# First token tile turned by TensorE instead of by the DMA: the first 15 microseconds of a matmul-bound kernel

## Chip, cores, metric

One core of one Trainium2 chip. The metric is the device time of one execution in microseconds (us), median over several runs; the kernel before takes 486.51 us (486.48 to 487.02 in its first three runs).

## The reference, cut to what matters

```
x: [2048, 1024] bf16;  two blocks A and B, each with wqkv [1024, 3072] and wo [1024, 1024]
g = sigmoid((x * gate_w).sum(-1))
a = linear attention of x with A's weights;   b = dilated window attention of x with B's weights
out = g * a + (1 - g) * b
```

Everything starts from `x @ wqkv`. The matmuls of this kernel contract over partitions, so they need x transposed: 128 of the 1024 features in the partitions, tokens along the free axis. The input holds x by tokens.

## The kernel before

The program is a list of operations with costs and dependencies; a list scheduler places them and so fixes, before the run, the order of the instructions on every engine. At run time each engine works through its fixed order and waits for semaphores. What matters here is the opening: value projection of block B, token tile by token tile (tile t is 128 tokens), four tiles at a time: first with the left half (512 columns) of the value weights, then with the right half. Eight matmuls of 128x512 make one tile and half.

```python
    WARM = 11
...
        def load_x(t, prio):          # DMA transpose of one token tile, 256 KB, on the sync queue
            return P.op("sp", lambda e: e.dma_start_transpose(xT[:, :, t * 128:(t + 1) * 128], x2[e_, r * 128:(r + 1) * 128, :]),
                        1.5, writes=[...], prio=prio, chan="x%d" % t, lat=1.3)
        def load_w(slot, half, src, c0, prio, d0=0, d1=8, eng="sp", after=()):   # d0..d1: blocks of 128 rows, 128 KB each
            return P.op(eng, lambda e: e.dma_start(ws[slot][:, d0:d1, half * 512:half * 512 + 512], src[:, d0:d1, c0:c0 + 512]), ...)

        load_x(0, 0)
        load_w(0, 0, Bw, 2048, 0.1, 0, 2, "act")
        load_w(0, 0, Bw, 2048, 0.2, 2, 4, "act")
        load_w(0, 0, Bw, 2048, 0.3, 4, 6)
        load_w(0, 0, Bw, 2048, 0.4, 6, 8)
        for t in range(1, NT):
            load_x(t, 3 + t)
        for d in range(0, 8, 2):
            load_w(0, 1, Bw, 2560, 6.1 + 0.1 * d, d, d + 2)
...
        for i in range(WARM):         # matmuls on zeros, to get the TensorE clock released before data arrives
            P.op("pe", lambda e: e.matmul(banks[7].ap(), warm[:, 0:128], warm[:, :], start=True, stop=True), 0.43, ...)
...
            step = 2 if t == 0 else 8  # tile 0 starts on each weight pair as it lands
```

A "weight pair" below is one load of two 128-row blocks, 256 KB. There are four for the left half (two on ScalarE's DMA queue, two on the sync queue) and four for the right half (the "second half's pairs").

## Time and profile before

| | before |
|---|---|
| time, median | 486.51 us |
| span of the profiled run | 485.2 us |
| PE (TensorE) busy | 98% |
| first real matmul | 5.54 us |
| clock of PE released | 4.3 us |
| last pair of the second half landed | 15.02 us |

The first part of the page of before gives busy time, share of the span and number of instructions of each engine; its fourth part, the chain that ended last by engine:

```profile
PE 474.2 (98%) x4339; PEld 222.8 (46%) x4403; DVE 285.2 (59%) x547; ACT 140.2 (29%) x227; POOL 5.9 (1%) x36
...
PE 95%; SPq 2%; issue 1%; DMA 1%; ACT 0%; DVE 0%
```

The list of waits of PE in before, from 15.4 us to the end (what it waited for: us in total, times, longest):

```profile
PE ps_all L1334 <- issue: 3.5, 22, 0.2
PE ps_all L1334 <- DMA w<-in_B_wqkv_dram: 0.3, 1, 0.3
PE ps_all L1334 <- ACT e L1341: 0.2, 1, 0.2
```

Together they say that after the opening PE waits for nearly nothing: what is gained or lost at the start is gained or lost in the whole. The timeline of PE in before, first 20 us (start, duration, instruction, times, and the idle time before it with what ended it; line 1373 is the warm-up, 1334 the projections):

```profile
1.25 4.01 PE L1373 MATMUL ps_all<-warm 128*128 128x512 bf16 x11 [1.25 <-DVE warm L1283]
5.54 1.47 PE L1334 MATMUL ps_all<-w,xT 128*128 128x512 bf16 x6 [0.28 <-DMA xT<-in_A_x_dram]
7.25 0.60 PE L1334 MATMUL ps_all<-w,xT 128*128 128x512 bf16 x2 [0.24 <-DMA w<-in_B_wqkv_dram]
8.17 6.82 PE L1334 MATMUL ps_all<-w,xT 128*128 128x512 bf16 x30 [0.32 <-DMA xT<-in_A_x_dram]
15.30 4.91 PE L1334 MATMUL ps_all<-w,xT 128*128 128x512 bf16 x22 [0.30 <-DMA w<-in_B_wqkv_dram]
```

The clock is best seen in the weight loads of PE (one ahead of each matmul). While the clock is held at half rate they are listed one by one, 0.43 us apart; once it is released they run 0.216 us apart and are merged into one line. In before that happens at 4.2 to 4.4 us, still within the warm-up. The granted-clock column of the page (PEclk) reads 1.00 all the while and does not show it: the trace's own clock records begin only at the first release (4.24 us in before), and what lies ahead of the first record counts as 1.00.

```profile
3.36 0.15 PEld L1373 LDWEIGHTS ps_all<-warm 128*128 128x128 bf16 x1 [0.28 <-issue]
3.79 0.15 PEld L1373 LDWEIGHTS ps_all<-warm 128*128 128x128 bf16 x1 [0.28 <-issue]
4.22 0.55 PEld L1373 LDWEIGHTS ps_all<-warm 128*128 128x128 bf16 x3 [0.28 <-issue]
```

The timeline of the sync queue in before (times in which the queue was busy issuing):

```profile
0.80 1.38 SPq L1308 DMA_TRANSPOSE xT<-in_A_x_dram  x1
2.24 1.06 SPq L1313 DMA_DIRECT2D w<-in_B_wqkv_dram  x2
3.35 4.92 SPq L1308 DMA_TRANSPOSE xT<-in_A_x_dram  x3
8.31 2.12 SPq L1313 DMA_DIRECT2D w<-in_B_wqkv_dram  x4
```

Two more readings of before. First, one window from 3.0 to 5.5 us (busy time of PE, PEld, DVE, ACT, POOL with the number of instructions, then granted clock, DMA share, GB/s): the DMA moves 296 GB/s. Second, the first matmul behind the opening: the key and query projections (`ps_all<-xT,w`), which come after all 16 x 16 = 256 matmuls of the opening, start at 62.1 us.

```profile
3.00:5.50 2.50, 2.26 (x8) 0.70 (x6) 1.03 (x5) 0.06 (x1) 2.08 (x11) 1.00 1.10 296
...
L1334 PE MATMUL ps_all<-xT,w x745: 379/379/390, 62.1 to 389.4; 128*128 128x512 bf16 x187
```

That mark is the ruler of this study. To three digits it is 62.132 us in before. 256 matmuls at 0.2158 us (216 ns start to start, 10.74 us for 49 with the last one's tail) take 55.25 us, so PE stands at the mark as if it had started cleanly, at full rate and without a wait, at 62.13 - 55.25 = 6.89 us. This "clean start" takes in every wait and every slow matmul of the opening. From the mark to the end of the program all profiles of this study take 422.9 to 423.4 us.

### The profile page before, as it was taken

The page shows a single profiled execution, that of the slowest core. Times are in us where ns is not written, and L with a number is a line of the kernel's source. Part 1 is how long each engine was busy: PE and PEld are TensorE (multiplying, and loading weights), DVE is VectorE, ACT ScalarE, POOL GpSimd, SP SyncE. Part 2 cuts the span into 40 slices and gives each one's busy share as a digit, 9 for nine tenths or more (in the row PEclk, how much of TensorE's full clock was granted, in tenths as well). Part 3 has the DMA queues.
Part 4 walks back from the last instruction along what each step waited for, and adds up shares of the span by engine and source line. Part 5 has one row for each costly group of instructions (what it writes and reads, how often), then busy time and mean ns, then how long its engine had stood idle before and what let it go on. Part 6 is the DMA issues. An engine that isn't in the chain of part 4 may idle for free.

```text
span 485.2 us, 10105 instructions
## 1 busy us (share of the span) xinstructions
PE 474.2 (98%) x4339; PEld 222.8 (46%) x4403; DVE 285.2 (59%) x547; ACT 140.2 (29%) x227; POOL 5.9 (1%) x36
## 2 busy tenths in 40 slices
PE   8999999999999999999999999999999999999997
PEld 3444444444444444454544554444444444444443
DVE  2121435888688888665666556496579236653434
ACT  2111121235322234334443333455532230111000
POOL 4000000000000000000000000000000000000000
PEclk9999999999999999999999999999999999999999
DMA  8999993132014459433222322820086018830212
GB/s 224 222 194 299 309 355 122 65 110 86 1 44 135 107 138 245 100 76 86 55 75 67 85 66 66 204 54 2 10 217 163 1 15 242 221 24 2 88 68 89
DMA packets 72951, 57.39 MB, mean 118 GB/s; under 512 B 37953, under 2 KB 60865, under 8 KB 72898
## 3 DMA queue, kind: packets, MB, share of 16 engines
q1 hardware_dynamic: 72210, 56.07, 44.3%
q8 instruction: 36, 0.59, 0.5%
q10 hardware_dynamic: 688, 0.59, 0.4%
q14 instruction: 17, 0.14, 0.1%
HBM read 34.49 MB, written 13.76 MB: 99 GB/s over the span
## 4 chain that ended last, share of the span: by engine, by line
PE 95%; SPq 2%; issue 1%; DMA 1%; ACT 0%; DVE 0%
PE ps_all L1334 78%; PE ps_all L1693 11%; PE ps_all L1463 2%; PE ps_all L1440 2%; SPq L1308 1%; DMA w<-in_B_wqkv_dram 1%; PE ps_all L1556 1%; SPq L1313 1%; PE ps_all L1638 0%; PE ps_all L1610 0%; ACT e L1341 0%; DVE o L1697 0%
## 5 line engine op out<-in xcount | busy, mean ns | idle before, releaser
L1334 PE MATMUL ps_all<-w,xT 128*128 128x512 bf16 x924 | 208.6, 379 | 4.5 <-issue 2.1
L1334 PE MATMUL ps_all<-xT,w 128*128 128x512 bf16 x745 | 166.3, 379 | 2.2 <-issue 1.4
L1334 PEld LDWEIGHTS ps_all<-w,xT 128*128 128x128 bf16 x960 | 91.2, 98 | 111.1 <-DMA w<-in_B_wqkv_dram 2.1
L1334 PEld LDWEIGHTS ps_all<-xT,w 128*128 128x128 bf16 x768 | 73.9, 98 | 88.7 <-issue 1.3
L1693 PE MATMUL ps_all<-w,qT 128*128 128x512 bf16 (+1 forms) x260 | 55.4, 372 | 0.2
L1693 PEld LDWEIGHTS ps_all<-w,qT 128*128 128x128 bf16 x264 | 25.9, 98 | 29.6
L1365 DVE CAST vst<-ps_all 128x512 bf16<-128x512 f32 x15 | 10.4, 694 | 43.5 <-PE ps_all L1334 43.5
L1448 ACT ACTIVATE E<-ps_all 128x1824 bf16<-128x1824 f32 (+1 forms) x18 | 30.4, 1689 | 13.4 <-PE ps_all L1440 13.4
L1345 DVE TENSOR_SCALAR e<-e 128x512 bf16<-128x512 bf16 x64 | 18.4, 290 | 26.9 <-ACT e L1343 14.0
L1697 DVE SCALAR_TENSOR_TENSOR o<-ps_all,gm,xT 128x512 bf16<-128x512 f32 (+1 forms) x25 | 18.0, 728 | 21.1 <-PE ps_all L1693 20.8
L1341 ACT ACTIVATE e<-ps_all 128x512 bf16<-128x512 f32 x32 | 19.1, 598 | 39.0 <-PE ps_all L1334 38.1
L1343 ACT ACTIVATE e<-ps_all 128x512 bf16<-128x512 f32 x32 | 19.1, 598 | 32.3 <-PE ps_all L1334 32.3
L1295 DVE TENSOR_TENSOR mx<-mx,kT 128x1024 bf16<-128x1024 bf16 x32 | 20.9, 688 | 10.9 <-ACT kT L1366 10.8
L1295 DVE TENSOR_TENSOR mx<-mx,qT 128x1024 bf16<-128x1024 bf16 x32 | 20.8, 687 | 7.9 <-ACT qT L1369 7.9
L1451 DVE TENSOR_TENSOR E<-E,msk 128x1824 bf16<-128x1824 bf16 (+1 forms) x18 | 19.9, 1104 | 7.8 <-ACT E L1448 7.4
L1366 ACT ACTIVATE vst<-ps_all 128x512 bf16<-128x512 f32 x17 | 10.2, 601 | 48.5 <-PE ps_all L1334 45.1
L1480 DVE TENSOR_TENSOR ot<-ps_all,rs 128x512 bf16<-128x512 f32 x36 | 23.3, 686 | 0.0
L1366 ACT ACTIVATE az<-ps_all 128x512 bf16<-128x512 f32 x22 | 13.2, 601 | 34.5 <-PE ps_all L1334 34.5
L1366 ACT ACTIVATE kT<-ps_all 128x512 bf16<-128x512 f32 x20 | 11.9, 597 | 37.6 <-PE ps_all L1334 37.6
L1347 DVE SCALAR_TENSOR_TENSOR pk<-ps_all,e 128x512 bf16<-128x512 f32 x32 | 22.0, 689 | 0.7
L1369 ACT ACTIVATE qT<-ps_all 128x512 bf16<-128x512 f32 x19 | 11.4, 598 | 37.4 <-PE ps_all L1334 37.3
L1369 ACT ACTIVATE xT<-ps_all,g 128x512 bf16<-128x512 f32 x10 | 6.9, 689 | 45.1 <-PE ps_all L1334 45.1
(72 smaller groups left out, 260.2 us busy)
## 6 DMA issues: line engine op xcount, KB each, us to landing
rb<-rc_hbm SPq DMA_DIRECT2D x32, 256.0 KB, 5.2
w<-in_A_wqkv_dram SPq DMA_DIRECT2D x6, 1024.0 KB, 9.0
v<-vB_hbm SPq DMA_DIRECT2D x36, 132.0 KB, 2.7
vB_hbm<-vst SPq DMA_DIRECT2D x32, 132.0 KB, 6.2
w<-in_B_wqkv_dram SPq DMA_DIRECT2D x4, 1024.0 KB, 9.5
xn<-in_A_x_dram SPq DMA_DIRECT2D x16, 256.0 KB, 2.7
out_dram<-o SPq DMA_DIRECT2D x15, 256.0 KB, 2.1
oB_hbm<-ot SPq DMA_DIRECT2D x36, 96.0 KB, 2.2
```

Of the source, the lines that this page charges most:

```text
L1295: P.op("dve", lambda e, m=m, op=op: e.tensor_tensor(m[:, 0:n], m[:, 0:n], src, op), 0.08 + n / 1920.0, reads=[m.all(), reg], writes=[m.all()],
L1334: last = e.matmul(bank.ap(), lhs(dc), rhs(dc), start=(dc == 0), stop=(dc == 7))
L1341: P.op("act", lambda e: e.activation(e_[:, :], bank.ap(), ACT.Exp), act(512), reads=[bank.iv], writes=[e_.all()])
L1343: P.op("act", lambda e: e.activation(e_[:, :], bank.ap(), ACT.Exp, accum_out=qe[:, col:col + 1]), act(512) + 0.1, reads=[bank.iv], writes= ...
L1345: P.op("dve", lambda e: e.tensor_scalar(e_[:, :], e_[:, :], 1.0, 1e-6, op0=ALU.min, op1=ALU.add), 0.25, reads=[e_.all()], writes=[e_.all()])
L1347: P.op("dve", lambda e: e.scalar_tensor_tensor(out=dst, in0=bank.ap(), scalar=0.0, in1=e_[:, :], op0=ALU.max, op1=ALU.add), dps(512), read ...
L1366: fa = lambda e: e.activation(dst, src(), ACT.Copy)
L1369: fa = lambda e: e.activation(dst, src(), ACT.Copy, scale=scale)
L1448: P.op("act", lambda e: e.activation(E[:, 0:32 * nq].rearrange("p (j q) -> p j q", j=4), ps[:, 4:8, 0:8 * nq], ACT.Exp), act(32 * nq), rea ...
L1451: P.op("dve", lambda e: e.tensor_tensor(ev(), ev(), m[:, :, :].rearrange("p r q -> p (r q)")[:, None, :].to_broadcast([128, 16, 2 * nq]), ...
L1480: P.op("dve", lambda e, r=r, bv=bv, h=h: e.tensor_tensor(o[:, 512 * h:512 * h + 512].rearrange("p (k i c) -> p k i c", k=2, c=32), bv()[:, ...
L1693: last = e.matmul(bank.ap(0, f1 - f0), qT[:, dc, t * 128:(t + 1) * 128], ws[3][:, dc, f0:f1], start=(dc == 0), stop=(dc == 7))
```

## The change

Intent: do not wait for the slow DMA transpose of tile 0 (5.5 us). Load it by rows in two halves, plain loads at the front of ScalarE's queue, and turn it on TensorE with an identity (8 matmuls of 128 columns into PSUM, four copies by VectorE and ScalarE into `xT`). Tile 1's DMA transpose takes the freed place at the front of the sync queue. Warm-up shrinks from 11 matmuls to 4 and 2 more that fit in where the schedule has room. The rest is for the scheduler: it is told when loads land (`due`), from which it derives the fixed orders.

```diff
-    WARM = 11
+    WARM = 4
+    WARM2 = 2
...
+        def load_x0(lo, hi, prio, pad):
+            P.op("act", lambda e: e.dma_start(x0[:, lo:hi], x2[0, 0:128, lo:hi]), 0.45, ..., lat=None, pad=pad)
+        def due(o, cost, pad):
+            o.cost, o.lat, o.pad = cost, None, pad
-        load_x(0, 0)
-        load_w(0, 0, Bw, 2048, 0.1, 0, 2, "act")
-        load_w(0, 0, Bw, 2048, 0.2, 2, 4, "act")
-        load_w(0, 0, Bw, 2048, 0.3, 4, 6)
-        load_w(0, 0, Bw, 2048, 0.4, 6, 8)
-        for t in range(1, NT):
-            load_x(t, 3 + t)
+        load_x0(0, 512, 0, 1.75)
+        due(load_w(0, 0, Bw, 2048, 0.1, 0, 2, "act"), 0.45, 2.2)
+        load_x0(512, 1024, 0.2, 1.6)
+        due(load_w(0, 0, Bw, 2048, 0.3, 2, 4, "act"), 0.45, 2.1)
+        due(load_x(1, 0), 1.4, 3.9)
+        due(load_w(0, 0, Bw, 2048, 0.3, 4, 6), 0.5, 3.0)
+        due(load_w(0, 0, Bw, 2048, 0.4, 6, 8), 0.5, 3.7)
+        for t in range(2, NT):
+            o = load_x(t, 3 + t)
+            if t < 4:
+                due(o, 1.3, 3.5)
...
+        for p in range(4):            # turn two blocks at a time, copy them into xT
+            def turn(e, b=b, p=p):
+                for k in range(2):
+                    d = 2 * p + k
+                    last = e.matmul(b.ap(128 * k, 128 * k + 128), x0[:, d * 128:(d + 1) * 128], ident[:, :], ...)
+            P.op("pe", turn, 0.22, ...)
+            P.op("act" if p % 2 else "dve", fn, ...)
+        for i in range(WARM2):
+            P.op("pe", ... the same matmul on zeros ..., prio=-0.4)
...
-            step = 2 if t == 0 else 8
+            step = 2 if t == 0 or t == 1 and half == 0 else 8
```

(Cut: the identity built on POOL, and finer dependencies on parts of `xT`.)

More of the change, by code (lines that the diff above doesn't have):

```diff
@@ L188, in schedule @@
             if o.chan is not None:
-                dma_free = max(dma_free, o.end) + o.lat
-                fin = dma_free + o.pad
+                if o.lat is None:
+                    fin = o.end + o.pad
+                else:
+                    dma_free = max(dma_free, o.end) + o.lat
+                    fin = dma_free + o.pad
             o.pos = len(self.order[e])
@@ L1220, in build_kernel @@
     xn = Ring([SB([128, 1024], BF16, "xn%d" % i, at=az.t[i].lo) for i in range(2)])
+    x0 = SB([128, 1024], BF16, "x0", at=az.t[2].lo)
+    ident = SB([128, 128], BF16, "ident", at=az.t[3].lo)
     top_ = base[0]
@@ L1264, in C @@
             return P.op(eng, fn, cost, reads=reads, writes=writes, prio=-1)
+        C("pool", lambda e: e.memset(ident[:, :], 0.0), 0.1, [ident.all()])
+        C("pool", lambda e: e.affine_select(out=ident[:, :], in_=ident[:, :], compare_op=ALU.not_equal, fill=1.0, base=0, pattern=[[-1, 128]], channel_multiplier=1), 0.3,
+          [ident.all()], [ident.all()])
         for z in vst.t:
@@ L1314, in load_w @@
                         writes=[ws[slot].part((d0, d1), (half * 512, half * 512 + 512))], prio=prio, chan="w%d_%d_%d" % (slot, half, d0), lat=0.55 * n, after=after)
-        load_x(0, 0)
-        load_w(0, 0, Bw, 2048, 0.1, 0, 2, "act")
-        load_w(0, 0, Bw, 2048, 0.2, 2, 4, "act")
-        load_w(0, 0, Bw, 2048, 0.3, 4, 6)
-        load_w(0, 0, Bw, 2048, 0.4, 6, 8)
-        for t in range(1, NT):
-            load_x(t, 3 + t)
+        def load_x0(lo, hi, prio, pad):
+            P.op("act", lambda e: e.dma_start(x0[:, lo:hi], x2[0, 0:128, lo:hi]), 0.45, writes=[x0.part((lo, hi))], prio=prio, chan="x0_%d" % lo, lat=None, pad=pad)
+        def due(o, cost, pad):
[11 more added lines that the diff above has]
+                due(o, 1.3, 3.5)
         for d in range(0, 8, 2):
@@ L1373, in plan @@
             P.op("pe", lambda e: e.matmul(banks[7].ap(), warm[:, 0:128], warm[:, :], start=True, stop=True), 0.43, reads=[warm.all()], writes=[banks[7].iv], prio=-1)
+        for p in range(4):
+            b = banks[p]
+            def turn(e, b=b, p=p):
+                for k in range(2):
+                    d = 2 * p + k
+                    last = e.matmul(b.ap(128 * k, 128 * k + 128), x0[:, d * 128:(d + 1) * 128], ident[:, :], start=(k == 0), stop=(k == 1), skip_group_check=True)
+                return last
+            P.op("pe", turn, 0.22, reads=[x0.part((256 * p, 256 * p + 256)), ident.all()], writes=[b.iv], prio=-0.5 + 0.01 * p)
+            src = lambda b=b: b.ap(0, 256).rearrange("p (k s) -> p k s", k=2)
+            dst = xT[:, 2 * p:2 * p + 2, 0:128]
+            fn = (lambda e, dst=dst, src=src: e.activation(dst, src(), ACT.Copy)) if p % 2 else (lambda e, dst=dst, src=src: e.tensor_copy(dst, src()))
+            P.op("act" if p % 2 else "dve", fn, act(256) if p % 2 else dps(256), reads=[b.iv], writes=[xT.part((2 * p, 2 * p + 2), (0, 128))], prio=3 + 0.01 * p)
+        for i in range(WARM2):
+            P.op("pe", lambda e: e.matmul(banks[7].ap(), warm[:, 0:128], warm[:, :], start=True, stop=True), 0.43, reads=[warm.all()], writes=[banks[7].iv], prio=-0.4)
         early = {(2, 0): (1, 0, Bw, 1024, 21), (4, 1): (2, 0, Bw, 0, 22), (7, 1): (1, 1, Bw, 1536, 23), (10, 1): (2, 1, Bw, 512, 24),
@@ L1382, in plan @@
             w, wr = w_half(0, half)
-            step = 2 if t == 0 else 8
+            step = 2 if t == 0 or t == 1 and half == 0 else 8
             for d in range(0, 8, step):
-                o = group(bank, xs, w, [xr, ws[0].part((d, d + step), (half * 512, half * 512 + 512))], d, d + step)
+                o = group(bank, xs, w, [xT.part((d, d + step), (t * 128, (t + 1) * 128)), ws[0].part((d, d + step), (half * 512, half * 512 + 512))], d, d + step)
             move(vt[:, :, 0:32], lambda bank=bank: bank.ap().rearrange("p (h d) -> p h d", d=32), 512, bank, vt.part((0, 16), (0, 32)))
```

## The prediction

> **What bounds the kernel now.** TensorE. The page's first part has PE busy 474.2 of 485.2 us (98%), the chain of waits lies 95% on PE, and the list of PE's waits after 15.4 us holds only short issue gaps (3.5 us in 22 pieces) and one wait for ScalarE of 0.2 us. So only the first 15 us can win. There the timeline of PE shows 11 warm-up matmuls from 1.25 to 5.26 us, then broken pieces: 6 matmuls from 5.54, 2 from 7.25, 30 from 8.17, and an unbroken run from 15.30. Matmuls start 0.216 us apart (0.427 until 4.3 us, where the clock is released). 38 precede 15.30, so PE stands as if it had started cleanly at 15.30 - 38 x 0.216 = 7.1 us. The change can move this "clean start".
>
> **Who sets it.** Landings in the trace: first weight pair 3.6, second 5.3, token tile 0 (DMA transpose) 5.5, third and fourth pair 6.4 and 7.2, tiles 1 to 3 at 8.1, 9.1, 10.2, the second half's pairs at 11.5, 12.6, 14.3, 15.0. The last ends the last wait (the chain runs through the sync queue's issues up to 9.96, then 5.07 us of weight DMA). The DMA engines are near full from 2.5 us, except for a dip (195 GB/s in the 8 to 10 us window): the second half's weights were issued only from 8.31, behind four transposes that cost the queue 1.25 to 2.27 us each.
>
> **What the change does.**
> - Takes one DMA transpose off the sync queue: tile 1's starts there at 0.8 instead of 3.35, and everything behind is issued about 1.3 to 2.3 us earlier. This fills the dip.
> - Puts two more issues on ScalarE's queue (about 0.45 us each); the activation-table load (1.28 us) slips to about 2.7 to 4.0.
> - Adds 8 TensorE turns (128 columns, about 0.11 us cold each), four copies out of PSUM (estimate 0.4 us, from the 0.6 to 0.7 us of 512 columns) and an identity on POOL; drops 5 warm-up matmuls. All lies where PE waited. 256 KB go as 1 KB packets (46 ns each) instead of 256 B ones (18 to 25 ns): about 0.3 us less DMA time.
>
> **Estimate.** Tile 0's halves land at about 3.0 and 4, turned and copied by 4.5; weight pairs at about 4, 5.2, 6.1, 7.0; tile 1 at 5.5, tiles 2 and 3 at 8.2 and 9.4; second-half pairs to 12.7 to 13.8. First real matmul about 4.6. Clean start by each landing (landing + 0.27 - 0.216 per matmul ahead of it): third pair 5.5, tile 2 5.0, last second-half pair 4.8 to 5.9. The worst, about 5.7, is 1.4 us before today's 7.1, all on the critical path: no later wait of PE could swallow it.
>
> The risk is the clock. The Trainium skill ("TensorE: Matmul & The Clock Gate", Part 1, What's actually happening) says it is released after one busy window of about 3.4 us, free-running; this trace agrees (3.05 us after the first matmul). With gaps between warm-ups and turns a window may be missed, which would cost about 1 us of the gain.
>
> **Predicted: 485.1 us, 8 in 10 between 484.2 and 486.3.** Faster by over 2%: 0.01; within 2%: 0.98; slower: 0.01.
>
> **Right if** the first real matmul starts near 4.6, tile 1 lands before 6, second-half weights are issued from about 6.5 and the last lands by 13.8, and the unbroken run starts correspondingly. **Wrong if** matmuls stay 0.427 us apart past 5 us; if the copies queue on VectorE behind mask copies that wait for POOL, or on ScalarE behind the table load, so that the first matmul starts after 5.5; or if the last second-half pair still lands near 15 (gain about nil).

## The result, and the profile after

After takes 490.09 us in the median of six runs (488.87 to 491.37); before, run beside it, 486.60. The ratio is 1.0069, 95% interval 1.0052 to 1.0086: slower by 0.7%. (Ratios are the mean time of one kernel's fast runs over that of the other's of the same rounds, so not quite the ratio of the medians quoted.) The runs of after spread over 2.5 us, those of before over 0.5. The profiled run of after (488.87) happens to be its fastest.

The page of after, first and fourth part, as shown of before:

```profile
PE 474.8 (97%) x4342; PEld 223.5 (46%) x4406; DVE 286.3 (59%) x550; ACT 139.6 (29%) x228; POOL 6.2 (1%) x38
...
PE 97%; issue 1%; DMA 1%; ACT 0%; ACTq 0%; DVE 0%
```

PE's waits of after from 15.4 us on: nothing has come in there.

```profile
PE ps_all L1353 <- issue: 3.3, 21, 0.2
PE ps_all L1353 <- ACT qT L1388: 0.2, 1, 0.2
PE ps_all L1353 <- ACT e L1360: 0.2, 1, 0.2
```

The timeline of PE in after (1392 and 1409 are warm-up, 1401 the turns, 1353 the projections):

```profile
1.25 1.89 PE L1392 MATMUL ps_all<-warm 128*128 128x512 bf16 x4 [1.25 <-DVE warm L1292]
2.93 0.63 PE L1409 MATMUL ps_all<-warm 128*128 128x512 bf16 x1
3.36 0.63 PE L1401 MATMUL ps_all<-ident,x 128*128 128x128 bf16 x4
3.78 0.63 PE L1409 MATMUL ps_all<-warm 128*128 128x512 bf16 x1
6.69 0.61 PE L1401 MATMUL ps_all<-ident,x 128*128 128x128 bf16 x4 [2.27 <-DMA x<-in_A_x_dram]
7.09 13.28 PE L1353 MATMUL ps_all<-w,xT 128*128 128x512 bf16 x52
```

The first half of tile 0 is turned at 3.36 us. Then PE stands idle for 2.27 us, because the second half lands only at 6.65, and the first real matmul starts at 7.09, 1.55 us later than in before. The weight loads of PE in after tell of the clock:

```profile
8.66 0.15 PEld L1353 LDWEIGHTS ps_all<-w,xT 128*128 128x128 bf16 x1 [0.27 <-DVE msk L1288]
9.08 0.15 PEld L1353 LDWEIGHTS ps_all<-w,xT 128*128 128x128 bf16 x1 [0.28 <-issue]
9.51 0.15 PEld L1353 LDWEIGHTS ps_all<-w,xT 128*128 128x128 bf16 x1 [0.28 <-issue]
9.94 0.15 PEld L1353 LDWEIGHTS ps_all<-w,xT 128*128 128x128 bf16 x1 [0.27 <-issue]
10.28 0.75 PEld L1353 LDWEIGHTS ps_all<-w,xT 128*128 128x128 bf16 x4 [0.20 <-issue]
```

Real work goes at half rate (0.43 us) until 10.28 us. The sync queue of after:

```profile
0.80 1.38 SPq L1317 DMA_TRANSPOSE xT<-in_A_x_dram  x1
2.24 1.07 SPq L1322 DMA_DIRECT2D w<-in_B_wqkv_dram  x2
3.35 5.30 SPq L1317 DMA_TRANSPOSE xT<-in_A_x_dram  x2
8.70 2.12 SPq L1322 DMA_DIRECT2D w<-in_B_wqkv_dram  x4
```

There is one transpose less in front of the second half's pairs, yet they are issued at 8.70 instead of 8.31: the two remaining transposes take 5.30 us to issue (single records: 1.47 and 3.79), where before's three took 4.92. The window from 3.0 to 5.5 us and the mark, in after:

```profile
3.00:5.50 2.50, 1.42 (x7) 0.57 (x5) 0.93 (x4) 1.60 (x2) 1.05 (x5) 1.00 1.06 213
...
L1353 PE MATMUL ps_all<-xT,w x745: 379/379/390, 64.0 to 391.3; 128*128 128x512 bf16 x187
```

213 GB/s instead of 296, and the mark at 64.025 instead of 62.132: 1.89 us lost before it, of 1.96 us in the span. So nearly all of the loss of this run lies in the opening. The landings (the time at which a load's semaphore had its full count in the trace), in us:

| load | before | forecast | after |
|---|---|---|---|
| tile 0, first half / second half | 5.49 (transpose) | 3.0 / 4 | 3.01 / 6.65 |
| first, second pair (ScalarE's queue) | 3.58, 5.30 | 4, 5.2 | 6.25, 8.14 |
| third, fourth pair (sync queue) | 6.36, 7.21 | 6.1, 7.0 | 7.58, 8.91 |
| tile 1 | 8.13 | 5.5 | 6.45 |
| tiles 2, 3 | 9.14, 10.20 | 8.2, 9.4 | 9.77, 10.64 |
| second half's last pair | 15.02 | 12.7 to 13.8 | 15.12 |

Same bytes, later landings.

### The profile page after: what moved, and what is told of

Same layout as the page of the kernel before. It is cut to its first block, busy times and chain, and to the rows that moved or that the text cites. A ratio compares the mean times of both kernels' runs of the same rounds, so it can differ in the third digit from the quotient of the medians.

```text
span 487.1 us, 10117 instructions
## 1 busy us (share of the span) xinstructions
PE 474.8 (97%) x4342; PEld 223.5 (46%) x4406; DVE 286.3 (59%) x550; ACT 139.6 (29%) x228; POOL 6.2 (1%) x38
## 4 chain that ended last, share of the span: by engine, by line
PE 97%; issue 1%; DMA 1%; ACT 0%; ACTq 0%; DVE 0%
PE ps_all L1353 80%; PE ps_all L1729 11%; PE ps_all L1499 2%; PE ps_all L1476 2%; DMA x<-in_A_x_dram 1%; PE ps_all L1592 1%; PE ps_all L1674 0%; PE ps_all L1646 0%; ACT e L1360 0%; ACT qT L1388 0%; PE ps_all L1401 0%; DVE o L1733 0%; ACTq L1322 0%; ACTq L1326 0%
## 5 line engine op out<-in xcount | busy, mean ns | idle before, releaser
L1466 DVE TENSOR_SCALAR qd<-qT,par 128x912 bf16<-128x912 bf16 (+1 forms) x35 | 15.0, 453 | 9.6 <-PE ps_all L1476 9.2
```

## The experiments

Two theories. **Clock theory**: the loss is that PE's gap lets the clock stay at half rate long into the real work. **Data theory**: the loss is that the data comes later. They do not exclude each other; the runs are to size them. All kernels gave correct results. The table has the clean start of each profile (its mark less 55.25 us), the DMA rate of its window from 3.0 to 5.5 us, and the times.

| run | clean start | GB/s | median, us | ratio to before, 95% interval |
|---|---|---|---|---|
| before | 6.89 | 296 | 486.5 | 1 |
| after | 8.78 | 213 | 490.09 | 1.0069 (1.0052 to 1.0086) |
| e1 fill | 8.17 | 220 | 488.53 | 1.0036 (1.0019 to 1.0052) |
| e2 before, 4 warm-ups | 7.66 | 308 | 488.28 | 1.0033 (1.0016 to 1.0051) |
| e3 tile 1 behind weights | 11.61 | 341 | 492.11 | 1.0113 (1.0094 to 1.0131) |
| e4 both halves first | 9.32 | 193 | 489.36 | 1.0056 (1.0039 to 1.0073) |
| e5 before with row loads | 9.77 | 230 | 490.37 | 1.0063 (1.0037 to 1.0089) |
| e6 tiles swapped | 8.94 | 211 | 489.56 | 1.0066 (1.0045 to 1.0088) |
| e7 before, tile 3 last | 6.89 | 309 | 487.01 | 0.9999 (0.9985 to 1.0013) |
| e8 plain loads first | 6.78 | 316 | 487.58 | 1.0015 (1.0001 to 1.0028) |
| e9 one queue | 7.81 | 282 | 488.89 | 1.0054 (1.0040 to 1.0068) |
| e10, e11 after again | 10.10, 9.82 | 227, 194 | 489.96, 489.77 | one run each |
| e12 before, split loads | 7.51 | 219 | 487.34 | 1.0010 (0.9995 to 1.0025) |
| e13 before, merged loads | 7.09 | 297 | 487.76 | 1.0018 (1.0004 to 1.0032) |
| e14 after, merged loads | 9.45 | 176 | 487.94 | 1.0026 (1.0012 to 1.0039) |
| e15 one queue, merged | 6.63 | 330 | 486.87 | 1.0011 (0.9997 to 1.0024) |
| e16 the same, more warm-up | 7.14 | 302 | 487.20 | 1.0007 (0.9993 to 1.0020) |
| e17 before, 128 + 384 KB | 6.78 | 274 | 487.50 | 1.0012 (0.9995 to 1.0028) |
| e18 before, 384 + 128 KB | 7.21 | 262 | 487.34 | 1.0001 (0.9985 to 1.0018) |

A clean start is one profile, and so is a DMA rate. Landings vary from run to run: e15 and e16 issue the same early loads at the same times, yet the first weights came 0.9 us apart, at 330 and 302 GB/s. The profiled run was the slowest of its kernel in e12, e14, e16 and e18, and the fastest in after, e9, e15 and e17. The time of a run exceeds its span by 1.7 to 1.8 us in most kernels, but by 2.0 to 2.1 in e1, e3 and e9 (and in most runs of e8 and e16); why is not known, so for these the spans are the better measure of the opening. Differences under 0.3 us are not read below.

### The clock: e1, e2, e10, e11

**e1.** Six more warm-up matmuls between the turns of the two halves, where PE idled.

```diff
+            if p == 1:
+                for i in range(6):
+                    P.op("pe", lambda e: e.matmul(banks[7].ap(), warm[:, 0:128], warm[:, :], start=True, stop=True), 0.1, ..., prio=-0.6, after=[o])
```

> After, with six more warm-up matmuls on TensorE between the turn of the first half of tile 0 and that of the second, where the profile of after has 2.27 us of idle PE. Clock theory (the loss is that PE's idle gap lets the clock stay at half rate until 10.3 us): matmuls are 0.216 us apart by 7.5 us, the clean start falls from 8.8 to 7.1 to 7.6, time 486.6 to 487.6. Data theory (the loss is the late landing of tile 0's second half and of the weights alone): the second half lands at 6.6 as before and the time stays 489 to 491.

Measured: 488.53 us (488.19 to 488.70), the spread down from 2.5 to 0.5 us. In the weight loads of PE the clock is released at 5.55 us, long before the first real matmul:

```profile
4.70 0.15 PEld L1406 LDWEIGHTS ps_all<-warm 128*128 128x128 bf16 x1 [0.28 <-issue]
5.13 0.15 PEld L1406 LDWEIGHTS ps_all<-warm 128*128 128x128 bf16 x1 [0.28 <-issue]
5.55 0.10 PEld L1406 LDWEIGHTS ps_all<-warm 128*128 128x128 bf16 x1 [0.28 <-issue]
```

The time lies between the two forecasts: of the 0.69% that after loses, the filling gives back 0.33 points, about 1.6 us; 0.36%, about 1.75 us, stay. But some 0.35 us of what stays lies outside the span: by spans, the six runs of after stand about 3.3 us above before and e1 1.4 us, so the filling gave back 1.9 us. The data was late as before (second half 6.93, second pair 8.46):

```profile
7.64 0.59 PE L1353 MATMUL ps_all<-w,xT 128*128 128x512 bf16 x2
8.60 15.70 PE L1353 MATMUL ps_all<-w,xT 128*128 128x512 bf16 x72 [0.36 <-DMA w<-in_B_wqkv_dram]
```

With the clock out of the way, PE waits for the second weight pair: (8.46 + 0.05) less two matmuls ahead of it gives a clean start of 8.08; measured 8.17, which is 1.28 us behind before. So each theory has a large share: by spans about 1.9 us for the clock and 1.4 for the data.

**e2.** Before with `WARM = 4` and nothing else.

> Before, with 4 warm-up matmuls in place of 11 and nothing else. Clock theory: PE idles from about 3.0 to 5.5 us, the clock is released only at about 9 to 12 us, and the time rises to 487 to 488.5 with a wider spread than before's 0.5 us. Data theory: landings do not change, so 486.6.

Measured: 488.28 us (487.82 to 488.75), slower than before by 0.33%. Landings as in before (tile 0 at 5.47). PE idles from its last warm-up until 5.51 and works at half rate until 10.02 us:

```profile
9.33 0.15 PEld L1334 LDWEIGHTS ps_all<-w,xT 128*128 128x128 bf16 x1 [0.28 <-issue]
9.76 1.23 PEld L1334 LDWEIGHTS ps_all<-w,xT 128*128 128x128 bf16 x6 [0.27 <-issue]
```

The clock theory is borne out in time; the spread (0.9 us) is wider than before's, as forecast. In the profiled run, the second fastest of four, the clean start moved by 0.77 us only; the mean loss by spans is 1.55 us.

**e10, e11.** After unchanged, twice.

> After unchanged, for a second profile. Six runs of after spread over 2.5 us (before: 0.5). Clock theory: the landings repeat within 0.5 us and the first real matmul starts at 7 to 7.5 again, but the release of the clock falls anywhere from 10 to 13.3 us, and the span is longer by half the delay. Data theory: the release stays near 10.3 and what differs are the landings.

> After unchanged, for a third profile; the same is expected as of the second.

The weight loads of PE, first of e10, then of e11:

```profile
12.23 0.15 PEld L1353 LDWEIGHTS ps_all<-w,xT 128*128 128x128 bf16 x1 [0.28 <-issue]
12.66 0.77 PEld L1353 LDWEIGHTS ps_all<-w,xT 128*128 128x128 bf16 x4 [0.28 <-issue]
```

```profile
11.65 0.15 PEld L1353 LDWEIGHTS ps_all<-w,xT 128*128 128x128 bf16 x1 [0.28 <-issue]
11.97 0.96 PEld L1353 LDWEIGHTS ps_all<-w,xT 128*128 128x128 bf16 x5 [0.17 <-issue]
```

The first matmul at full rate starts at 12.90 and 11.97 us, in after's first profile at 10.28. Landings repeat within 0.6 us (second half 6.45 and 7.01, second pair 8.30 and 8.58; after: 6.65 and 8.14). With the number of real matmuls that had gone by then, the release alone gives the clean start, and the split of the loss follows: "by data" is where the second pair's landing (plus 0.05, less two matmuls) would have put it at full rate.

| profile | release | matmuls before it | release - 0.2158 x matmuls | clean start by the mark | lost to data | lost to the clock |
|---|---|---|---|---|---|---|
| after | 10.28 | 7 | 8.77 | 8.78 | 0.87 | 1.02 |
| e10 | 12.90 | 13 | 10.09 | 10.10 | 1.02 | 2.19 |
| e11 | 11.97 | 10 | 9.81 | 9.82 | 1.30 | 1.63 |

The release makes most of after's spread (1.2 us between the last column's extremes, 0.4 us between those of the data), and the first profile had caught a lucky one. The Trainium skill ("TensorE: Matmul & The Clock Gate", Part 1, What's actually happening) calls the window of about 3.4 us free-running, "it doesn't reset when your kernel starts"; releases at 10.3, 12.0 and 12.9 us in one and the same program agree. e11 shows the steps themselves. By the clock records of its trace the clock had been released at 5.02 us, was taken back at 8.43, after PE had waited for data, and came again at 11.85: twice 3.41 us. Two windows of e11 (columns as above; the figure after POOL's, 1.00 and 0.50, is the granted clock):

```profile
5.02:8.43 3.41, 0.83 (x6) 0.34 (x6) 0.85 (x2) 0.38 (x1) 0.92 (x6) 1.00 1.21 296
8.43:11.85 3.42, 3.14 (x8) 1.17 (x9) 0.62 (x3) 0.00 (x0) 1.36 (x7) 0.50 1.05 220
```

So late data cost clock in two ways: it kept the release away (after), or it made PE lose a release that it had (e11, and e4 and e5 below).

### The data: e3, e4, e5, e6

**e3.** Tile 1's transpose behind the third and fourth pair.

```diff
-        due(load_x(1, 0), 1.4, 3.9)
+        due(load_x(1, 0.5), 1.4, 3.9)
```

> After, with tile 1's transpose put behind the third and fourth weight pair on the sync queue. Data theory (tile 1's transpose, started first, takes DMA time from tile 0 and its weights): tile 0's second half lands by 5.5 instead of 6.65 and the first weight pair by 4.5 instead of 6.25, the first matmul starts about 5.5; the time falls to 487 to 489. Clock theory: the gap shortens from 2.3 to about 1 us, so the clock may or may not be released early; time anywhere from 487 to 490. If landings do not move, the transpose is not what delays them.

Measured: 492.11 us, the slowest, and outside both forecasts. The second half came at 6.36 (not by 5.5), though until 5.28 only plain loads were in flight, at 341 GB/s from 3.0 to 5.5: the sync queue's pairs got more than their half (third pair 4.31, fourth 5.78; first pair 5.32). Then tile 1's transpose met the last pair of ScalarE's queue: the two, 512 KB, took until 9.75 and 9.60, the DMA fell to 97 to 222 GB/s from 6.5 to 9.5 us, and PE stood until 9.74; then the clock stayed at half rate until 14.4. The transpose is not what delayed the second half here. Its meeting with the other queue's plain load was slow at this later place too, though not every such meeting is: before has one from 3.0 to 5.5, at 296 GB/s.

**e4.** Both halves ahead of the first pair on ScalarE's queue.

```diff
-        load_x0(512, 1024, 0.2, 1.6)
+        load_x0(512, 1024, 0.05, 1.6)
```

> After, with both halves of tile 0 issued on ScalarE's queue before the first weight pair. Data theory (place in the queue): tile 0's second half lands at about 4.2 instead of 6.65, but the first weight pair is then the last to come, at 6 or later, so the first matmul starts at about 6.5 and PE idles about as long; time 488.5 to 490.5. Clock theory says the same for the time, as PE again idles for about 2 us before its first real matmul.

Measured: 489.36 us, as forecast, but the second half landed at 5.90 (not 4.2) and the first pair at 7.18. Place in the queue explains only part. The clock was released at 4.42 us, taken back at 7.83 and released again at 11.24, as in e11.

**e5.** Before with the two row loads added where after has them, their data unused; tile 0 still comes by transpose.

```diff
         load_x(0, 0)
+        load_x0(0, 512, 0.05)
+        load_x0(512, 1024, 0.15)
         load_w(0, 0, Bw, 2048, 0.1, 0, 2, "act")
```

> Before, with the two row loads of tile 0 added on ScalarE's queue in the places where after has them (first, and between the two weight pairs); what they load is not used, tile 0 still comes by its transpose, first on the sync queue. In after the plain 1 KB packets of ScalarE's queue took 150 to 280 ns each between 3 and 5 us, where before's took 46. If the row loads on the other queue cause that (they put the two queues out of step), it is seen here too: first weight pair at 5.5 or later, tile 0 at 6 or later, time 487.5 to 489. If it comes from transposing tile 1 instead of tile 0 first, the packets stay at 46 to 60 ns and all lands later only by the 256 KB more, about 0.8 us: time 487 to 487.5.

Measured: 490.37 us. First pair 6.19 (before: 3.58), tile 0's transpose 6.38, second pair 8.75; 230 GB/s. In size this is after's loss, without a turn or an identity, from 256 KB more in two loads. It is more than forecast, and not data alone: in spite of 11 warm-ups the clock, released at 4.82 us, was taken back at 8.24 while PE waited for the second pair, and PE worked at half rate until 11.65.

```profile
4.82:8.24 3.42, 1.32 (x6) 0.23 (x3) 0.73 (x4) 0.00 (x0) 1.58 (x8) 1.00 1.22 298
8.24:11.65 3.41, 2.86 (x7) 1.03 (x8) 0.00 (x0) 0.08 (x1) 0.00 (x0) 0.50 0.99 202
```

Worked out as in the table above, the clean start lost 1.48 us to the data and 1.41 to the clock. The times fit: three of the four runs list a mean granted clock of 0.992 to 0.997 and took 490.03 to 491.28 us; the fourth, at 1.000, took 488.26, 1.5 us more than before. The 1 KB packets of ScalarE's queue took 60 to 99 ns on average per half microsecond. The 150 to 280 ns that the forecast gives for after were not typical either: from 3 to 5 us only 15% of after's packets lie there; three quarters took 51 ns or less, and the mean was 78.

**e6.** Tile 1 by rows and TensorE, tile 0 by transpose at the front (addresses exchanged in the loads, the copies and `load_x`).

> After, with the roles of the two tiles exchanged: tile 1 goes by rows and TensorE, tile 0 by the transpose at the front of the sync queue. If it matters which rows are transposed first, the plain packets fall back to about 46 ns, the first weight pair lands near 4 and the row half near 5, time 487 to 488. If it is the mix of row loads and a transpose, all is as in after: pair at 6.2, second half at 6.6, time 489 to 491.

Measured: 489.56 us; first pair 6.46, second half 6.93, 211 GB/s, all as in after. Which rows are transposed does not matter.

### What makes the DMA slow: e12, e13, e14, e17, e18

**e12.** Before, its two pairs on ScalarE's queue issued as four loads of one block. Same bytes, packets and order.

```diff
-        load_w(0, 0, Bw, 2048, 0.1, 0, 2, "act")
-        load_w(0, 0, Bw, 2048, 0.2, 2, 4, "act")
+        for d in range(4):
+            load_w(0, 0, Bw, 2048, 0.1 + 0.05 * d, d, d + 1, "act")
```

> Before, with the two weight pairs on ScalarE's queue issued as four loads of 128 KB instead of two of 256 KB: same bytes, same packets, same order. If four smaller loads on that queue beside a transpose are what made after's loads slow (number and size, not the rows of tile 0), the second pair lands at 6 or later instead of 5.3, tile 0's transpose too, and the time rises to 487.5 to 489. If it was the added bytes or the row loads themselves, the pairs land within 0.5 us of before's 3.6 and 5.3, and the time stays at 486.6 to 487.2.

The window from 3.0 to 5.5 us of e12:

```profile
3.00:5.50 2.50, 2.50 (x8) 0.84 (x6) 1.02 (x5) 1.22 (x1) 2.08 (x11) 1.00 1.12 219
```

219 GB/s against before's 296. The last of the four loads lands at 7.28 (before: 5.30), the fourth pair at 8.22 (7.21), tile 1 at 9.17 (8.13). The landings are what the number-of-loads theory forecast; the time is not: 487.34, not resolved from before (interval 0.9995 to 1.0025), as the clean start moved by 0.6 us only. The profiled run (487.82) is the slowest of four; but its 219 GB/s stand apart from the 296 to 309 of the four profiles with two loads of 256 KB, or one of 512, on that queue.

**e13.** Before with pairs merged two by two (one load of four blocks on each queue, two for the second half).

```diff
-        load_w(0, 0, Bw, 2048, 0.1, 0, 2, "act")
-        load_w(0, 0, Bw, 2048, 0.2, 2, 4, "act")
-        load_w(0, 0, Bw, 2048, 0.3, 4, 6)
-        load_w(0, 0, Bw, 2048, 0.4, 6, 8)
+        load_w(0, 0, Bw, 2048, 0.1, 0, 4, "act")
+        load_w(0, 0, Bw, 2048, 0.3, 4, 8)
```

> Before with its weight pairs merged two by two: one 512 KB load on ScalarE's queue, one on the sync queue, and two for the second half. Number-of-loads theory: the DMA runs at 300 GB/s or more throughout, tile 0 and the first four weight blocks land by 5.3, the other four by 7.0, tile 1 by 7.9; the clean start is 6.2 to 6.7 against 6.9, time 0.2 to 0.7 us below before. Otherwise: no change or, as two pairs land as one, 0.2 us slower.

Measured: 487.76 us, 0.2% slower; 297 GB/s; tile 0 at 5.58, weights 4.56 and 7.54. Fewer loads than before do not make it faster.

**e14.** After with tile 0 as one load of 256 KB, weights merged as in e13, and more warm-up.

```diff
-        load_x0(0, 512, 0, 1.75)
-        due(load_w(0, 0, Bw, 2048, 0.1, 0, 2, "act"), 0.45, 2.2)
-        load_x0(512, 1024, 0.2, 1.6)
-        due(load_w(0, 0, Bw, 2048, 0.3, 2, 4, "act"), 0.45, 2.1)
+        load_x0(0, 1024, 0, 2.0)
+        due(load_w(0, 0, Bw, 2048, 0.1, 0, 4, "act"), 0.5, 4.0)
```

> After with tile 0 as one load of 256 KB, the weights as in e13, and PE kept busy (5 warm-up matmuls before the turns, 6 behind), so that the clock is no issue. Number-of-loads theory: tile 0 lands at 3.6 to 4.0 (as the first weight pair of before), the first four weight blocks by 6.2, tile 1 by 6.2, the other four by 7.8; first real matmul at about 6.3; clean start 6.3 to 7.0, time 486.0 to 486.8 (e1, the same with four loads: 488.5). If not the number: tile 0 after 5, weights after 7.5, time 488 or more.

Two loads on ScalarE's queue, and the slowest window of all:

```profile
3.00:5.50 2.50, 1.23 (x9) 0.69 (x8) 0.57 (x3) 0.04 (x1) 0.85 (x4) 1.00 0.99 176
```

Tile 0 landed at 4.70 (its first of 16 parts at 3.17), the weights at 8.35, tile 1 at 8.55. PE idled again and the clock was released at 10.5 us only, so the run did not take the clock out as planned either. By time (487.94 us, forecast 486.0 to 486.8; fastest run 487.55) the number-of-loads theory missed its forecast. The profile weighs less: its run, 489.65 us, is the slowest of five by 1.4 us, and tile 0's packets were slow (205 ns on average from 2.0 to 2.5 us, 98 in e15) before the first packet of a transpose at 2.85. So the theory is not confirmed as a full explanation, and not refuted either.

**e17, e18.** Sorted by rate, the slow profiles seemed to be those whose first load on ScalarE's queue was over just as the transpose's packets began (about 2.6 us). So before was run with the 512 KB divided 128 + 384 and 384 + 128.

> Before, with the 512 KB on ScalarE's queue divided 128 + 384 instead of 256 + 256. Boundary theory: the first load is over at 2.6 us as the transpose starts, the second starts late and the DMA runs at 180 to 235 GB/s between 3 and 5.5 us (before: 296); the 512 KB and tile 0 are complete at 6 to 7 instead of 5.5, tile 1 lands 0.5 to 1 us later than 8.1. Otherwise: 280 GB/s or more and landings within 0.3 us of before's. Time 486.6 to 488.

> Before, with the 512 KB on ScalarE's queue divided 384 + 128. Boundary theory: the boundary lies at about 4 us, the queue flows when the transpose starts, and the DMA runs at 285 to 310 GB/s between 3 and 5.5 us; all as in before, 486.5 to 487. If any unequal division is slow: 180 to 235 GB/s as in e17.

Measured: 274 and 262 GB/s, 512 KB complete at 5.57 and 6.08, tile 1 at 8.12 and 8.53, times 487.50 and 487.34. The small load first is not slow. That theory fell too.

What the runs do show: with a transpose on the sync queue from the start, ScalarE's queue with one or two weight loads runs at 262 to 309 GB/s (before, e2, e7, e13, e17, e18); with four loads, whether of weights alone (e12) or with row loads (after, e1, e4, e5, e6, e10, e11), at 193 to 230; with one row load and one weight load (e14, its slowest run), at 176. Why is open.

### Looking for a version that wins: e7, e8, e9, e15, e16

**e7.** Before with tile 3's transpose behind the second half's pairs.

```diff
-            load_x(t, 3 + t)
+            load_x(t, 6.9 if t == 3 else 3 + t)
```

> Before, with one change: the four weight pairs of the second half are issued ahead of tile 3's transpose. They are then issued from about 7.0 instead of 8.3 us and fill the dip of the DMA at 9.5 us; tile 3 is needed only after 48 matmuls. The clean start is then set by tile 1 (8.17 - 8 x 0.216 = 6.4) instead of the last pair (7.1): 0.3 to 0.8 us less than before, 485.8 to 486.4. If the DMA takes as long for the pairs with tile 4 in place of tile 3 behind them, the last pair still lands near 15 and nothing is won.

Measured: 487.01 us, ratio 0.9999. The pairs were issued from 7.37 and the last landed at 13.23 instead of 15.02, yet the clean start stayed at 6.89. In this run tile 1 landed at 8.55 (8.13) and with 8 matmuls ahead set the clean start: 8.59 - 8 x 0.216 = 6.87. The forecast gain was partly an error in reading before: see below.

**e8.** After, plain loads ahead of all transposes: both halves and the second pair on ScalarE's queue; first, third, fourth pair, then tiles 1, 2, the second half's pairs and tile 3 on the sync queue; 6 warm-ups.

> After, reordered so that no transpose is in flight with plain loads: both halves of tile 0 and the second weight pair on ScalarE's queue, the first, third and fourth pair on the sync queue, then tiles 1 and 2 by transpose, then the second half's pairs, then tile 3; 6 warm-up matmuls before the turns and 2 behind. If the mix of transposes and plain loads is what made after late, the plain packets take 46 to 60 ns, tile 0 is complete by 4, the first pair by 4.3, all four by 6.2, tile 1 by 7.2, the first matmul starts at 4.8 to 5.2 with the clock at full rate by 5.5, the clean start is 5.2 to 6.2 and the time 485 to 486. If row loads are slow by themselves, tile 0 is complete only after 5.5 and the time is 486.5 or more.

Measured: 487.58 us. 316 GB/s and packets of 46 to 63 ns on ScalarE's queue, as the first branch said, but all four pairs by 7.14 (not 6.2) and tile 0 complete only at 5.07 (not 4), as e3 had shown of a share between two busy queues, and the first real matmul at 5.78. The clean start of 6.78 was set by the last pair of the second half (13.19).

**e9.** All early loads on the sync queue in the order of need.

> After, with every early load on the sync queue in the order of need: both halves of tile 0, the four weight pairs, tiles 1 and 2 by transpose, the second half's pairs, tile 3; nothing on ScalarE's queue; 5 warm-up matmuls before the turns. If the two queues side by side are what delayed tile 0 and its weights, all lands in order at 340 GB/s: tile 0 by 3.2, pairs at 3.9, 4.7, 5.4, 6.2, tile 1 at 7.2; the first real matmul starts at 4.6 to 5.1, PE never idles over 0.5 us, the clock is released by 7.7 at the latest, the clean start is 5.3 to 6.4 against 6.9 of before, and the time is 485.2 to 486.4. If one queue alone can't feed the DMA engines, the pairs land no earlier than in before and the time is 486.6 or more.

Measured: 488.89 us. Tile 0 at 3.39, first pair 4.57, second 5.27, and the first real matmul at 4.71: what the change had aimed at. But third and fourth pair came at 6.59 and 7.44, and the first store of results, which the schedule had put among the second half's pairs, held up the queue: the last pair was issued at 9.68 and landed at 14.22.

**e15.** e9 with tile 0 in one load, weights in loads of four blocks, and the store behind them.

```diff
+        load_x0(0, 1024, 0, 1.7)
+        due(load_w(0, 0, Bw, 2048, 0.2, 0, 4), 0.5, 2.9)
+        due(load_w(0, 0, Bw, 2048, 0.4, 4, 8), 0.5, 3.9)
+        for t in range(1, NT):
+            o = load_x(t, (1, 1.1, 1.4)[t - 1] if t < 4 else 3 + t)
...
+        for d in range(0, 8, 4):
+            load_w(0, 1, Bw, 2560, 1.2 + 0.01 * d, d, d + 4)
```

> e9 with tile 0 as one load, weights as 512 KB loads, all on the sync queue in the order of need, and all of the second half's weights and tile 3 issued before the first store. Number-of-loads theory: tile 0 at 3.0 to 3.3, first four blocks by 4.9, the other four by 6.4, tile 1 by 7.4, tile 2 by 8.4, second half by 11.5; first real matmul at 5.0; clean start 5.6 to 6.4 against 6.9; time 485.2 to 486.2, the version that beats both. If e9 was slowed only by the store among its loads: the same within 0.3 us. If neither: as e9, 488 or more.

Measured: 486.87 us against 486.58 of before beside it, ratio 1.0011 (0.9997 to 1.0024): the best version of the change, and no better than before. Tile 0 at 3.81, weights 5.26 and 6.98, tile 1 at 7.98; the two transposes took 4.60 us to issue, so the second half left at 6.91 and ended at 12.61, which set the clean start of 6.63.

**e16.** e15 with 7 warm-ups before and 3 behind the turns.

> e15 with 7 warm-up matmuls before the turns and 3 behind, so that PE is busy from 1.25 to the first real matmul without a gap of more than 0.2 us. Clock theory: the spread of the runs shrinks from 1.3 to about 0.5 us, the landings stay (tile 0 at 3.8, weights 5.3 and 7.0, tile 1 at 8.0, second half 12.6), the clean start stays at 6.6 against 6.9 of before, and the time is 486.2 to 486.7, before less 0.1 to 0.4. If the spread comes from the landings, it stays above 1 us.

Measured: 487.20 us, spread 0.64 instead of 1.31 us, as the clock theory said. But the landings were later in this profile, the slowest of its five runs (first four blocks 6.19, the rest 7.49), the clean start 7.14, and the ratio 1.0007. No version beat before.

## Why the prediction was wrong, point by point

- *"What bounds the kernel", "only the first 15 us can win"*: right. Of the profiled loss of 1.96 us, 1.89 lie before the mark.
- *"Tile 0's halves land at about 3.0 and 4 ...; weight pairs at about 4, 5.2, 6.1, 7.0"*: this step failed. I took the DMA's rate of before (about 300 GB/s) and "same bytes" for granted and let the second half overtake what stands before it. Measured 3.01 and 6.65; pairs 6.25, 8.14, 7.58, 8.91; the rate 213 GB/s. Worth 0.9 to 1.3 us by the table of e10 and e11, about 1.4 us by the spans of e1. e5 (256 KB more) and e12 (the same bytes) show that loads beside a transpose alone do this; e3, e4 and e8 that part of it is plain sharing of the DMA between two queues.
- *"The risk is the clock ... about 1 us of the gain"*: the mechanism was right, the size too small, and it belonged into the sum, not behind it. I thought of one missed window; the cost was 1.0 to 2.2 us in three profiles and about 1.9 us by the spans of e1 (1.6 by the times), and e2 shows 1.6 us (0.33%) for the shortened warm-up alone. "Matmuls stay 0.427 us apart past 5 us" stood among the "wrong if" conditions, and came true. (The 3.05 us that the prediction calls agreement is a little less than a whole window; the steps of 3.41 us in e4, e5 and e11 are the better check.) PE's order is fixed before the run: when data is late, nothing fills the gap.
- *"Everything behind is issued about 1.3 to 2.3 us earlier. This fills the dip"*: failed. The second half's pairs were issued at 8.70 instead of 8.31, because the issue of a transpose stretches (3.79 us for tile 3). This is the first failed step again: in all 20 profiles the second of the first two transposes in a row ended its issue close to the landing of the load ahead of both, from 0.4 us before it to 0.2 after (seen together, not tested by a change), and that load, here the fourth pair, landed at 8.91 instead of 7.0. Their last landing stayed near 15, which the prediction had named as a case of "gain about nil"; it did not even come to bind.
- *"Clean start 7.1"*: a misreading. The matmul of the last pair in before started at 15.07, 0.05 us after its landing, like all others (8.128 to 8.173, 7.207 to 7.253); its record is missing from the trace, and I took the next one, at 15.30. So the clean start was 6.89, and the "0.27 us" from landing to matmul were 0.05. This is also why e7's expected gain shrank.
- *Copies behind mask copies or the table load*: harmless. The first copy ran at 3.81 us on VectorE and 4.23 on ScalarE; the second half's data came later than either.

The predicted 485.1 us, from a clean start of 5.7, stood against 490.09 us, from clean starts of 8.8 to 10.1.

## What to carry to other kernels

Before you move loads between queues, ask not only how many bytes there are but what flows beside them: the bytes stayed, and the landing of what was needed first moved by 2.7 us. If a change makes PE wait for data, count the clock into the sum: cut warm-up only where the data is sure to come, and place filler matmuls where the wait falls (warm-up ahead of the wait is not enough: e5 lost the clock in spite of 11). And judge a kernel whose times spread more than its neighbour's from several profiles; one may be its luckiest.

## What the Trainium skill lacked or had wrong

- "DMA: Bandwidth & Descriptors" (Issuing engines are not separate DMA queues) says that issuing from several engines only saves issue time. It does not tell that, with both queues at work, the number of loads on one can matter: beside a transpose on the sync queue, four loads on ScalarE's queue instead of two, same bytes, went with 219 instead of 296 GB/s between 3.0 and 5.5 us (e12, one profile each), and the row loads with 213 (after). The cause is open (e14, e17, e18).
- The same page (Rules for kernel authors) says "A transpose next to ordinary DMAs needs nothing". For correctness all runs agree; for speed see the point above.
- The same page (DMA Transpose) does not tell that a transpose can hold its issuing queue: 1.25 to 1.38 us for a transpose in most places, but 3.79 us in after and 4.23 us in e11 for the second of two in a row, until about the landing of the load ahead of both (8.66 and 8.91 us in after, 8.87 and 9.14 in e11).
- "TensorE: Matmul & The Clock Gate" (Part 1) agrees with these runs: full rate begins at 4.3 us in before, at 10.3, 12.0 and 12.9 us in three runs of after. It puts the ramp at under 1% of a kernel; here a shortened warm-up cost 0.33% (e2), more than many a change wins.
- Part 1 of that page does not say how busy PE must be within a window to keep the clock. Here it was taken back after PE had been busy 1.32 us of 3.42 (e5, no gap over 1.7 us) and 0.83 of 3.41 (e11).
- No page that I used tells that a profile's mean granted clock can read 1.00 while the matmuls run 0.427 us apart (after, 8 to 10 us, ahead of the first clock record at 10.19); the distance of the weight loads shows it.
